# One attention, MoE and soft-MoE kernel: the decoding of w_out spread over two chunks, and a mask, a maximum and a scaling made one instruction

## The chip, the cores and the metric

The kernel runs on one core of one Trainium2 chip. TensorE (PE, with its weight loads shown apart as PEld), VectorE (DVE), ScalarE (ACT), GpSimd (POOL) and SyncE (SP, which here only issues DMAs) each work through their own list of instructions in order and meet at semaphores. The metric is the device time of one launch in microseconds, as the median of several runs.

## The reference, cut to what matters

Three stages follow each other, and the output of each is the input of the next:

```python
# 1. attention with a forget gate: B=4, H=8, S=576, D=64
scores = q @ k.T / sqrt(D)
cum = cumsum(log(clip(f, 1e-4, 1)))
scores = where(causal, -1e9, scores + cum[:, None] - cum[None, :])
attn = exp(scores - max(scores)); attn /= sum(attn) + 1e-9
x = attn @ v                           # as 2304 tokens x 512
# 2. MoE layer 1: w_in 512 x 2048, w_out 2048 x 512
h = x @ w_in
x = (h * sigmoid(1.702 * h)) @ w_out
# 3. soft MoE: phi 512 x 32; 8 experts of 4 slots, F = 1024
logits = x @ phi
d = softmax(logits, over tokens); slot_in = d.T @ x
slot_out = relu(slot_in @ w1[e]) @ w2[e]        # per expert
out = softmax(logits, over slots) @ slot_out
```

w_in and w_out arrive as 64-bit floats and are read as pairs of 32-bit words.

## The kernel before, in words

**Order.** The program is written with tiles from named pools; a tile that takes the place of an older one of the same tag waits until that one's last reader is done. A scheduler then sets the order of the instructions on each engine, from the program's order and its own model of durations, so that a change in pools or program order moves instructions on every engine.

**Attention** is cut into 20 rows: 4 batches by 5 blocks of queries, four of 128 queries and a last one of 64. Rows 0 to 4 (the first batch) find their maxima beforehand (`emit_max`, `emit_mrow`, whose transposed maxima go to the PSUM tile mT and by ACT L411 into the operand qa). Rows 5 to 19 are *late rows* (`emit_qk`): the block of scores `scs` in PSUM gets the causal mask by a DVE addition in place (L333), its maximum by a DVE reduction (L537), for the rows of 64 queries the larger of that and the diagonal block's maximum (L541), and the maximum is scaled, with its sign turned, by L542. ACT then takes the exponential `pf` (L545) and its f16 part (L554), DVE the remainder (L555). Both parts, `pn`, are turned by a DMA transpose into `ph`, and PE multiplies them with the values (pv, L594 to L596). There are 78 such units: 6, 12, 24 and 24 of the rows whose width is 1, 2, 3 and 4 blocks (a unit holds 4, 2, 1 and 1 heads), and 12 of the rows of 64 queries. DVE L608 scales to x, and x is turned to `xt` (L640 on ACT, L641 on DVE).

**Layer 1** goes over 9 chunks of 256 tokens, each of 8 *units* (`moe_steps`): 12 matmuls `hp` (L746 to L748), a tanh on ACT (L754), a DVE instruction (L755) to `g`. w_out is never multiplied with all tokens: it is folded with phi first (`fold_phi`: w_out's tile is transposed to woT, copied by ACT L234, multiplied with phi to wps by L237, copied by DVE L241 to wphi), and a `turn` makes logits from g: four transposes gT (L722), an ACT copy (L724), four matmuls p (L726). At the end of a chunk `slot_steps` gathers the slots (lg, d of L818, sp of L826).

**Decoding of a weight tile.** Raw words land in SBUF, POOL (L194) or ACT (L196) takes the high word, ACT (L197) the low one, and DVE joins them by L199 and L202. The 32 tiles (16 of w_in, 16 of w_out) are asked for by `more_w`, up to five tiles ahead in DMAs.

**After the attention** the expert weights (128 tiles of 256 KB) stream through a ring of SBUF slots.

Of the kernel before, what the change touches and what calls it, by code (L numbers as in the profile page):

```python
# [30 lines left out]
def attention_moe_softmoe(ctx, tc, q, k, v, f, w_in, w_out, phi, w1, w2, out):  # L31
# [192 lines left out]
    w_phi, wps = [], {}  # L224

    def fold_phi(ff):

# [7 lines left out]
        o = wps[0][:, ff % 4 * NS:(ff % 4 + 1) * NS]  # L235
        for kk in range(KD):
            nc.tensor.matmul(  # L237
                o, lhsT=wt_[:, kk * 128:(kk + 1) * 128], rhs=phi_sb[:, kk, :], start=(kk == 0), stop=(kk == KD - 1)
            )
        if ff % 4 == 3:  # L240
            nc.vector.tensor_copy(  # L241
                wphi[:, ff - 3:ff + 1, :], wps[0][:, 0:4 * NS].rearrange("p (f s) -> p f s", f=4)
            )
# [234 lines left out]
    def emit_diag(r):  # L478
# [21 lines left out]
        nc.vector.tensor_reduce(out=m2, in_=dg, axis=AX.X, op=ALU.max)  # L500
        DG[r] = dg, m2

    def emit_qk(r, u):
# [33 lines left out]
        nc.vector.tensor_reduce(  # L537
            out=mx, in_=sc[:, 0:hb * nb].rearrange("p (h n) -> p h n", h=hb), axis=AX.X, op=ALU.max
        )
# [618 lines left out]
```

## Time and profile before

| quantity | value |
|---|---|
| time, median of 3 runs | 623.53 us (618.25 to 632.64) |
| span of the profiled execution | 615.8 us; its own time is not printed |
| lowest and median time above that span | 2.45 and 7.73 us |
| PE busy | 533.6 us (87%) |
| DVE busy | 377.4 us (61%) |
| ACT busy | 308.6 us (50%) |
| POOL busy | 67.9 us (11%) |

The page's span is what the profiler saw of one execution from the first instruction to the last, and the time of a run holds some microseconds around it. The program falls into stages: up to 64 us the loads and the first attention rows; 64 to 160 the first chunk of layer 1 with the folding of w_out; 160 to 465 the late attention rows with chunks 1 to 6; 465 to 545 the end of layer 1; 545 to the end the experts. The engine's busy time is read by stage, since each stage has another limit.

### The profile page before, as it was taken

The numbers are of one execution on the slowest core, as the hardware profiler recorded it, in microseconds if no ns is written. First come the engines' busy times: TensorE is split into PE (matmuls) and PEld (weight loads), VectorE is DVE, ScalarE is ACT, GpSimd is POOL, SyncE is SP. The second block draws the span as 40 slices with busy tenths as digits, with TensorE's granted clock in tenths as the row PEclk, the third lists the DMA queues.
The fourth block names the chain that finished last, engine by engine and source line by source line (L and its number), as shares of the span: only waits on it lengthen the run. The fifth ranks groups of instructions, "written<-read, shape, count | busy, mean of one in ns | idle before, by whom it ended". The sixth has DMA issues, their size and how long they took to land.

```text
span 615.8 us, 13848 instructions
## 1 busy us (share of the span) xinstructions
PE 533.6 (87%) x5447; PEld 335.1 (54%) x5447; DVE 377.4 (61%) x971; ACT 308.6 (50%) x603; POOL 67.9 (11%) x120
## 2 busy tenths in 40 slices
PE   4477979899889899979999989988999999879971
PEld 3376667688545555655556565555664544323541
DVE  8989586649575767787586875777754352320131
ACT  5776384657654556656466564555652342211120
POOL 4756272120000000000000000000000000000000
PEclk9887998899989989989999998999998999869996
DMA  9966685439993536999744897955451399689999
GB/s 252 249 161 144 181 263 155 142 102 154 189 173 79 94 74 122 173 183 185 141 82 70 139 163 164 152 80 104 79 91 22 117 381 322 206 278 351 285 279 280
DMA packets 246497, 105.65 MB, mean 172 GB/s; under 512 B 202624, under 2 KB 234112, under 8 KB 246432
## 3 DMA queue, kind: packets, MB, share of 16 engines
q1 hardware_dynamic: 246432, 104.77, 73.6%
q8 instruction: 43, 0.70, 0.5%
q14 instruction: 22, 0.18, 0.1%
HBM read 64.63 MB, written 4.72 MB: 113 GB/s over the span
## 4 chain that ended last, share of the span: by engine, by line
PE 42%; DMA 8%; DVE 2%; ACT 1%; issue 1%; SPq 1%; DVEq 0%; ACTq 0%
PE hp L746 6%; PE hp L747 6%; PE hp L748 6%; PE gT L722 4%; DMA ph<-pn 4%; PE sp L826 3%; DMA we<-in_moe_w_dram 3%; PE l L1055 2%; PE p L726 2%; PE pv L594 2%; PE so L1077 1%; PE scs L516 1%; PE scs L517 1%; PE pv L595 1%; PE pv L596 1%; PE sw L857 1%
## 5 line engine op out<-in xcount | busy, mean ns | idle before, releaser
L746 PE MATMUL hp<-w,xt 128*128 128x512 f16 x288 | 111.3, 386 | 0.0
L747 PE MATMUL hp<-w,xt 128*128 128x512 f16 x288 | 110.6, 384 | 0.0
L748 PE MATMUL hp<-w,xt 128*128 128x512 f16 x288 | 109.9, 382 | 0.0
L754 ACT ACTIVATE g<-hp 128x512 f32<-128x512 f32 x72 | 42.7, 593 | 75.4 <-PE hp L748 75.3
L755 DVE SCALAR_TENSOR_TENSOR g<-g,hp 128x512 f32<-128x512 f32 x72 | 49.1, 682 | 46.5 <-ACT g L754 46.2
L545 ACT ACTIVATE pf<-scs,mx 128x512 f32<-128x512 f32 (+3 forms) x108 | 54.8, 544 | 37.2 <-DVE mx L542 32.2
L555 DVE TENSOR_TENSOR pn<-pf,pn 128x512 f16<-128x512 f32 (+2 forms) x78 | 51.0, 655 | 25.3 <-ACT pn L554 24.8
L594 PE MATMUL pv<-vv,ph 128*128 128x65 f16 (+2 forms) x360 | 48.2, 201 | 11.0 <-DMA ph<-pn 6.9
L554 ACT ACTIVATE pn<-pf 128x512 f16<-128x512 f32 (+2 forms) x78 | 47.3, 608 | 17.3 <-DMA ph<-pn 16.1
L537 DVE TENSOR_REDUCE mx<-scs 128x1 f32<-128x512 f32 (+3 forms) x78 | 49.9, 642 | 3.0 <-PE scs L533 2.3
L722 PE MATMUL gT<-ident,g 128*128 128x128 f32 x288 | 48.3, 287 | 1.1 <-DVE g L755 1.1
L746 PEld LDWEIGHTS <-xt 128*128 128x128 f16 x288 | 28.6, 99 | 35.8 <-issue 13.9
L595 PE MATMUL pv<-vv,ph 128*128 128x65 f16 (+2 forms) x360 | 47.3, 198 | 0.0
L594 PEld LDWEIGHTS <-ph 128*128 128x128 f16 (+2 forms) x360 | 35.0, 103 | 22.4 <-DMA ph<-pn 9.0
L596 PE MATMUL pv<-vv,ph 128*128 128x65 f16 (+2 forms) x360 | 46.9, 196 | 0.0
L748 PEld LDWEIGHTS <-xt 128*128 128x128 f16 x288 | 28.4, 99 | 33.6 <-issue 2.8
L724 ACT COPY gt<-gT 128x512 f32<-128x512 f32 x72 | 41.6, 582 | 7.5 <-PE gT L722 7.2
L516 PE MATMUL scs<-kab,qa 128*128 128x128 f16 x240 | 36.7, 225 | 6.2 <-ACT pf L545 5.6
L747 PEld LDWEIGHTS <-xt 128*128 128x128 f16 x288 | 28.6, 99 | 23.0 <-issue 2.1
L722 PEld LDWEIGHTS gT<-ident,g 128*128 128x128 f32 x288 | 34.0, 145 | 11.8 <-issue 4.2
L595 PEld LDWEIGHTS <-ph 128*128 128x128 f16 (+2 forms) x360 | 35.5, 104 | 3.3 <-issue 0.4
L517 PE MATMUL scs<-kab,qb 128*128 128x128 f16 x240 | 36.5, 226 | 0.0
(198 smaller groups left out, 1048.6 us busy)
## 6 DMA issues: line engine op xcount, KB each, us to landing
we<-in_moe_w_dram SPq DMA_DIRECT2D x128, 256.0 KB, 5.5
raw<-in_moe_w_in_dram SPq DMA_DIRECT2D x16, 512.0 KB, 6.4
raw<-in_moe_w_out_dram SPq DMA_DIRECT2D x16, 512.0 KB, 4.6
kf<-in_k_dram SPq DMA_DIRECT2D x16, 256.0 KB, 3.5
qf<-in_q_dram SPq DMA_DIRECT2D x16, 256.0 KB, 4.2
out_dram<-ob SPq DMA_DIRECT2D x16, 256.0 KB, 4.0
vf<-in_v_dram SPq DMA_DIRECT2D x12, 256.0 KB, 3.6
ph<-pn SPq DMA_TRANSPOSE x78, 3.3
```

The source lines that it names most:

```text
L537: nc.vector.tensor_reduce(out=mx, in_=sc[:, 0:hb * nb].rearrange("p (h n) -> p h n", h=hb), axis=AX.X, op=ALU.max)
L545: nc.scalar.activation(out=pf[:, hh * nb:(hh + 1) * nb], in_=sc[:, hh * nb:(hh + 1) * nb], func=AF.Exp, bias=mx[:, hh:hh + 1], scale=SC,)
L554: nc.scalar.activation(out=pn[:, 0, 0:w], in_=pf, func=AF.Copy)
L555: nc.vector.tensor_tensor(out=pn[:, 1, 0:w], in0=pf, in1=pn[:, 0, 0:w], op=ALU.subtract)
L594: nc.tensor.matmul(o, lhsT=ph[0:rr, 0, off:off + n], rhs=vh, start=(j == 0), stop=False)
L595: nc.tensor.matmul(o, lhsT=ph[0:rr, 0, off:off + n], rhs=vl, start=False, stop=False)
L596: nc.tensor.matmul(o, lhsT=ph[0:rr, 1, off:off + n], rhs=vh, start=False, stop=(j == i))
L722: nc.tensor.transpose(pt[:, a * 128:(a + 1) * 128], g[:, a * 128:(a + 1) * 128], ident)
L746: first = nc.tensor.matmul(hp, lhsT=xt[:, 0, kk, ts], rhs=win(0, fg, kk), start=(kk == 0), stop=False)
L747: nc.tensor.matmul(hp, lhsT=xt[:, 0, kk, ts], rhs=win(1, fg, kk), start=False, stop=False)
L748: nc.tensor.matmul(hp, lhsT=xt[:, 1, kk, ts], rhs=win(0, fg, kk), start=False, stop=(kk == KD - 1))
L755: nc.vector.scalar_tensor_tensor(out=g, in0=g, scalar=1.0, in1=hp, op0=ALU.add, op1=ALU.mult)
```

## The change

- *w_out.* Chunk 0 asks for four weight tiles per unit up to its fourth unit as before (16 tiles, all of w_in), and from there for two per unit: 18, 20, 22, 24. Units 0 to 3 of chunk 1 ask for the other eight, two each. Loads are issued up to 7 tiles ahead rather than 5.
- *Turns* may begin as soon as the four tiles of w_out that they need are folded (`folded`), rather than when all are.
- *Folding* gathers two tiles: wps lies in the three `mm` buffers of PSUM rather than in the single `mi` one, and 8 copies of 128x64 to wphi take the place of 4 of 128x128. mT moves to `mm` as well.
- *SBUF.* w_out's decoded tiles lie in eight pairs o0 to o7 (the same bytes as before). Some raw tiles of w_out land in pairs that are still empty (`RAW_AT`) rather than in the ring `g`; the first rows' k and q lie in o7 to o5; the low words have a ring of two of their own, `low`, where they shared `gt` of three.
- *Late rows.* One DVE instruction per head (`tensor_tensor_reduce`, L556 of the new kernel) adds the mask, scales by minus 1/8 and takes the minimum, writing the scaled scores back in place and the minimum to mx; for the rows of 64 queries it starts from the diagonal's maximum, which `emit_diag` has scaled. It replaces L333, L537, L541 and L542. The mask becomes a tile `zmq` of 128x640, zeros ahead of the causal part. The exponential is taken with scale -1, pn's f16 part with the factor 256 by ACT, and its remainder by a DVE scalar_tensor_tensor (L569) rather than a tensor_tensor.

The core of the diff:

```diff
-    W_AHEAD = 5
+    W_AHEAD = 7
+    N_LOW = 2
+    RAW_AT = (7, 6, 5, 4, 3, None, None, 7, 6, None, None, 7, None, None, None, None)
...
-            raw = w_raw[n] = mp.tile([128, c], src.dtype, tag="g", name="raw", bufs=N_G)
+            at = None if which == "in" else RAW_AT[a]
+            if at is None:
+                raw = w_raw[n] = mp.tile([128, c], src.dtype, tag="g", name="raw", bufs=N_G)
+            else:
+                raw = w_raw[n] = wp.tile([128, c], src.dtype, tag=f"o{at}", name="raw")
...
-        low = mp.tile([128, 512], U32, tag="gt", name="low", bufs=N_GT)
+        low = ap_.tile([128, 512], U32, tag="low", name="low", bufs=N_LOW)
...
-        if ff % 4 == 0:
-            wps[0] = ps_mi("wps")
...
+        wot.append(wt_)
+        if len(wot) < 2:
+            return
+        wps = ps_mm("wps")[:, 0:2 * NS].rearrange("p (f s) -> p f s", s=NS)
...
+        nc.vector.tensor_copy(wphi[:, ff + 1 - 2:ff + 1, :], wps)
+        wot.clear()
+        folded[0] = (ff + 1) // 4
...
-        pt = ps_mi("mT")
+        pt = ps_mm("mT")
...
-            if r >= 5:
-                mask_in(sc[:, 0:w].rearrange("p (h n) -> p h n", h=hb)[:, :, 128 * i:], mqk)
...
-        nc.vector.tensor_reduce(
-            out=mx, in_=sc[:, 0:hb * nb].rearrange("p (h n) -> p h n", h=hb), axis=AX.X, op=ALU.max
-        )
-        if n < 128:
-            nc.vector.tensor_tensor(out=mx, in0=mx, in1=DG[r][1][:, u], op=ALU.max)
-        nc.vector.tensor_scalar(out=mx, in0=mx, scalar1=-SC, scalar2=math.log(PB), op0=ALU.mult, op1=ALU.add)
+        mask = zmq[:, 640 - nb:640] if n == 128 else zmq[:, 0:nb]
...
+            nc.vector.tensor_tensor_reduce(
+                out=o, in0=o, in1=mask, scale=-SC, scalar=3.0e38 if n == 128 else DG[r][1][:, u],
+                op0=ALU.add, op1=ALU.min, accum_out=mx[:, hh:hh + 1],
+            )
...
-        nc.scalar.activation(out=pn[:, 0, 0:w], in_=pf, func=AF.Copy)
-        nc.vector.tensor_tensor(out=pn[:, 1, 0:w], in0=pf, in1=pn[:, 0, 0:w], op=ALU.subtract)
+        nc.scalar.activation(out=pn[:, 0, 0:w], in_=pf, func=AF.Copy, scale=PB)
+        nc.vector.scalar_tensor_tensor(
+            out=pn[:, 1, 0:w], in0=pf, scalar=PB, in1=pn[:, 0, 0:w], op0=ALU.mult, op1=ALU.subtract
+        )
...
-            if c == 0:
-                more_w(max(6, 4 * u + 4))
+            if c < 2:
+                more_w((max(6, 4 * u + 4) if u < 4 else 16 + 2 * (u - 3)) if c == 0 else 24 + 2 * u + 2)
...
-            if w_at[0] == NW:
-                for _ in range(min(3 if c < 2 else 2, len(turns) - 1)):
-                    turn(*turns.popleft())
+            for _ in range(min(3 if c < 2 else 2, len(turns) - 1)):
+                if turns[0][2] >= folded[0]:
+                    break
+                turn(*turns.popleft())
```

How the order of instructions moves is shown at three places. On DVE in the late rows, before, at two heads of width 4 (g is of layer 1):

```order
L755 SCALAR_TENSOR_TENSOR g<-g,hp 128x512
L333 TENSOR_TENSOR scs<-scs,mqk 128x128
L537 TENSOR_REDUCE mx<-scs 128x1
L542 TENSOR_SCALAR mx<-mx 128x1
L333 TENSOR_TENSOR scs<-scs,mqk 128x128
L537 TENSOR_REDUCE mx<-scs 128x1
L555 TENSOR_TENSOR pn<-pf,pn 128x512
L542 TENSOR_SCALAR mx<-mx 128x1
```

The same engine in the same rows now (the instruction is listed as ISA; a second one, which reads the accumulated minimum to mx, follows it):

```order
L771 SCALAR_TENSOR_TENSOR g<-g,hp 128x512
L556 ISA scs,mx<-scs,zmq 128x512
L556 ISA mx 128x1
L793 TENSOR_SCALAR l_2656<-p_2188 128x256
L619 TENSOR_SCALAR rd<-pv 128x4
L622 RECIPROCAL rd<-rd 128x4
L569 SCALAR_TENSOR_TENSOR pn<-pf,pn 128x512
L556 ISA scs,mx<-scs,zmq 128x512
L556 ISA mx 128x1
```

Three instructions of a unit have become two that always stand together; nothing stands between maximum and scaling any longer.

On PE in chunk 0, before, between attention and two of layer 1's units (woT and wps are w_out's folding):

```order
L589 MATMUL pv<-vv,pf 128x65 x16
L232 MATMUL woT<-ident,w_1183 128x128 x4
L232 MATMUL woT<-ident,w_1191 128x128 x4
L237 MATMUL wps<-phi_sb,woT 128x32 x8
L232 MATMUL woT<-ident,w_1211 128x128 x4
L746 LDWEIGHTS xt
...
L237 MATMUL wps<-phi_sb,woT 128x32 x4
L232 MATMUL woT<-ident,w_1230 128x128 x4
L232 MATMUL woT<-ident,w_1338 128x128 x4
L237 MATMUL wps<-phi_sb,woT 128x32 x8
L232 MATMUL woT<-ident,w_1358 128x128 x4
L232 MATMUL woT<-ident,w_1378 128x128 x4
L746 LDWEIGHTS xt
```

PE in chunk 0 now, at two places ahead of a unit (scs is attention of the first batch):

```order
L252 MATMUL wps<-phi_sb,woT 128x32 x4
L243 MATMUL woT<-ident,wo 128x128 x4
L762 LDWEIGHTS xt
L762 MATMUL hp<-w,xt 128x512
...
L449 LDWEIGHTS kab
L449 MATMUL scs<-qa,kab 128x64
L451 LDWEIGHTS kab
L451 MATMUL scs<-qb,kab 128x64
L252 MATMUL wps<-phi_sb,woT 128x32 x8
L243 MATMUL woT<-ident,wo 128x128 x4
L762 LDWEIGHTS xt
L762 MATMUL hp<-w,xt 128x512
```

By the end of chunk 0's last unit 60 of the 64 woT transposes stood in the list before; now 32 do, and the other 32 follow in units 0 to 4 of chunk 1. The number of matmuls is the same.

On SP, before, around the first raw tiles of w_out (kab, qa and qb are attention's transposes):

```order
L179 DMA raw<-in_moe_w_in_dram 128x1024 x4
L181 DMA raw<-in_moe_w_out_dram 128x1024 x3
L312 DMA_TRANSPOSE qa<-qan 128x8x64
L312 DMA_TRANSPOSE qb<-qbn 128x8x64
L181 DMA raw<-in_moe_w_out_dram 128x1024 x3
L274 DMA qf<-in_q_dram 128x8x64
L312 DMA_TRANSPOSE qa<-qan 128x8x128
L312 DMA_TRANSPOSE qb<-qbn 128x8x128
L181 DMA raw<-in_moe_w_out_dram 128x1024 x2
L274 DMA qf<-in_q_dram 128x8x64
L181 DMA raw<-in_moe_w_out_dram 128x1024 x8
```

SP now, from the load of phi on:

```order
L119 DMA phi_sb<-in_moe_phi_dram 128x4x32
L195 DMA raw<-in_moe_w_out_dram 128x1024 x4
L193 DMA raw<-in_moe_w_in_dram 128x1024 x5
L195 DMA raw<-in_moe_w_out_dram 128x1024
L290 DMA qf<-in_q_dram 64x8x64
L328 DMA_TRANSPOSE kab<-kbn 128x8x128
L328 DMA_TRANSPOSE kab<-kan 128x8x128
```

The first four raw tiles of w_out now stand ahead of five raw tiles of w_in and of the third row's transposes, where they stood behind them.

## Rows read from the trace of the kernel before

**Rows 1.** Windows by stage: length; busy of PE, PEld, DVE, ACT, POOL; clock, DMA, GB/s.

```profile
0.00:64.00 64.00, 38.31 (x361) 33.69 (x362) 57.08 (x105) 42.45 (x68) 38.17 (x56) 0.84 0.82 197
64.00:160.00 96.00, 87.17 (x828) 68.95 (x826) 62.83 (x122) 57.80 (x110) 25.27 (x33) 0.95 0.69 172
160.00:465.00 305.00, 284.73 (x3089) 173.90 (x3089) 216.45 (x599) 175.18 (x353) 3.94 (x30) 0.96 0.70 124
465.00:545.00 80.00, 72.89 (x537) 34.77 (x536) 29.07 (x116) 23.64 (x55) 0.53 (x1) 0.91 0.67 230
545.00:615.80 70.80, 50.45 (x636) 23.75 (x636) 12.02 (x30) 9.50 (x19) 0.00 (x0) 0.89 0.99 288
```

**Rows 2.** PE's waits, 64 to 160 us: us in total, times, longest.

```profile
PE scs L433 <- ACT qa L411: 2.2, 1, 2.2
PE wps L237 <- ACT woT L234: 1.7, 3, 1.2
...
PE wps L237 <- DVE wphi L241: 0.5, 1, 0.5
...
PE mT L409 <- DVE wphi L241: 0.4, 1, 0.4
```

**Rows 3.** PE's waits, 160 to 470 us.

```profile
PE pv L594 <- DMA ph<-pn: 6.9, 7, 1.7
PE scs L516 <- ACT pf L545: 5.6, 3, 2.6
PE d L818 <- ACT dT L810: 3.9, 3, 2.5
PE pv L594 <- DVE x L608: 2.8, 2, 1.4
```

**Rows 4.** Windows of 4 us behind two long waits of PE.

```profile
216.00:220.00 4.00, 3.81 (x27) 2.25 (x31) 3.09 (x16) 3.08 (x9) 0.00 (x0) 0.50 0.49 92
...
272.00:276.00 4.00, 2.66 (x23) 2.34 (x23) 3.94 (x19) 4.00 (x13) 0.00 (x0) 0.50 1.00 189
```

**Rows 5.** DVE's groups by form, whole span: busy us, mean ns, idle before.

```profile
L555 DVE TENSOR_TENSOR pn<-pf,pn 128x512 f16<-128x512 f32 x42 | 28.8, 686 | 13.5 <-ACT pn L554 13.3
...
L537 DVE TENSOR_REDUCE mx<-scs 128x1 f32<-128x512 f32 x36 | 24.6, 685 | 2.7 <-PE scs L533 2.3
L333 DVE TENSOR_TENSOR scs<-scs,mqk 128x128 f32<-128x128 f32 x48 | 13.8, 291 | 6.6 <-PE scs L517 6.4
...
L537 DVE TENSOR_REDUCE mx<-scs 128x1 f32<-128x384 f32 x24 | 13.1, 546 | 0.2
...
L542 DVE TENSOR_SCALAR mx<-mx 128x1 f32<-128x1 f32 x60 | 8.7, 147 | 0.7
...
L333 DVE TENSOR_TENSOR scs<-scs,mqk 128x256 f32<-128x256 f32 x12 | 5.1, 426 | 0.1
L333 DVE TENSOR_TENSOR scs<-scs,mqk 128x512 f32<-128x512 f32 x6 | 4.2, 692 | 0.4 <-PE scs L517 0.4
...
L142 DVE TENSOR_TENSOR_SCAN cum<-ones,fs 32x576 f32<-32x576 f32 x1 | 1.3, 1346 | 0.8 <-ACT fs L139 0.8
```

**Rows 6.** Line L319, 160 to 470 us: count, ns as min/median/max, first and last start.

```profile
L319 DVE SCALAR_TENSOR_TENSOR vv<-vf,vv x12: 673/688/697, 162.1 to 394.4; 128x512 f16<-128x512 f32 x9, 64x512 f16<-64x512 f32 x3
```

**Rows 7.** Timeline of DVE, then of ACT, 210 to 214.5 us: start, duration.

```profile
212.62 0.15 DVE L542 TENSOR_SCALAR mx<-mx 128x1 f32<-128x1 f32 x1
...
211.14 0.63 ACT L287 ACTIVATE qbn<-qf 128x512 f16<-128x512 f32 x1 [2.10 <-DMA qb<-qbn]
...
212.61 0.58 ACT L754 ACTIVATE g<-hp 128x512 f32<-128x512 f32 x1
213.27 0.69 ACT L545 ACTIVATE pf<-scs,mx 128x512 f32<-128x512 f32 x1
```

**Rows 8.** Folding on PE, groups by form, 64 to 160 us.

```profile
L237 PE MATMUL wps<-phi_sb,woT 128*128 128x32 f32 x128 | 16.9, 279 | 2.2 <-ACT woT L234 1.7 <-DVE wphi L241 0.5
```

**Rows 9.** SP's waits in its queue, 0 to 165 us.

```profile
SPq L181 <- ACT low L197: 32.8, 12, 6.7
```

More of the change, by code (lines that the diff above doesn't have):

```diff
@@ L76, in attention_moe_softmoe @@
     ident16 = const.tile([128, 128], F16, name="ident16")
-    mqk = ap_.tile([128, 128], BF16, name="mqk")
+    zmq = ap_.tile([128, 640], BF16, name="zmq")
+    mqk = zmq[:, 512:640]
     mkq = ap_.tile([128, 128], BF16, name="mkq")
@@ L98, in setup_consts @@
         nc.vector.tensor_copy(identb, ident)
-        nc.gpsimd.memset(mqk, 0.0)
+        nc.gpsimd.memset(zmq, 0.0)
         nc.gpsimd.affine_select(
@@ L161, in attention_moe_softmoe @@
     w_at, w_loaded = [0], [0]
-    W_AHEAD = 5
+    W_AHEAD = 7
+    N_LOW = 2
+    RAW_AT = (7, 6, 5, 4, 3, None, None, 7, 6, None, None, 7, None, None, None, None)
+    wo_pair = {}
     def w32_tile(n):
-        return wp.tile([128, 512], F32, tag=f"w{n + 1 if n < NI else n}", name="w32")
+        if n < NI:
+            return wp.tile([128, 512], F32, tag=f"w{n + 1}" if n < NI - 1 else "o0", name="w32")
+        ff = n - NI
+        if ff % 2 == 0:
+            wo_pair[ff // 2] = wp.tile([128, 2, 512], F32, tag=f"o{ff // 2}", name="wo")
+        return wo_pair[ff // 2][:, ff % 2]
     def w_load(n):
@@ L222, in more_w @@
             fold_phi(*w_phi.pop())
-    w_phi, wps = [], {}
+    w_phi, wot, folded = [], [], [0]
     def fold_phi(ff):
-        if ff % 4 == 0:
-            wps[0] = ps_mi("wps")
         pt = ps_mm("woT")
@@ L234, in fold_phi @@
         nc.scalar.copy(out=wt_, in_=pt)
[L235 to L238, printed above, removed]
-            )
[L240 to L243, printed above, removed]
+        wot.append(wt_)
+        if len(wot) < 2:
+            return
+        wps = ps_mm("wps")[:, 0:2 * NS].rearrange("p (f s) -> p f s", s=NS)
+        for n, wt_ in enumerate(wot):
+            for kk in range(KD):
+                nc.tensor.matmul(
+                    wps[:, n], lhsT=wt_[:, kk * 128:(kk + 1) * 128], rhs=phi_sb[:, kk, :], start=(kk == 0), stop=(kk == KD - 1)
+                )
+        nc.vector.tensor_copy(wphi[:, ff + 1 - 2:ff + 1, :], wps)
+        wot.clear()
+        folded[0] = (ff + 1) // 4
     def split_one(n):
@@ L255, in attention_moe_softmoe @@
     ROW = {r: j for j, r in enumerate(rows)}
-    nat = {}
+    nat, first_kq = {}, {}
     KA, KB, QA, QB, VV = {}, {}, {}, {}, {}
@@ L268, in load_row @@
             elif r < 3:
-                t = wp.tile([128, H, D], F32, tag=f"w{2 * KF - 1 - 2 * r - (nm == 'q')}", name=nm + "f")
+                if r not in first_kq:
+                    first_kq[r] = wp.tile([128, 2, 512], F32, tag=f"o{7 - r}", name="kqf")
+                t = first_kq[r][:, nm == "q"].rearrange("p (h d) -> p h d", h=H)
             else:
@@ L500, in emit_diag @@
         nc.vector.tensor_reduce(out=m2, in_=dg, axis=AX.X, op=ALU.max)
+        nc.vector.tensor_scalar(out=m2, in0=m2, scalar1=-SC, scalar2=None, op0=ALU.mult)
         DG[r] = dg, m2
@@ L536, in emit_qk @@
         mx = ap_.tile([128, 4], F32, tag="mx", name="mx", bufs=4)[:, 0:hb]
[L537 to L542 removed]
+        mask = zmq[:, 640 - nb:640] if n == 128 else zmq[:, 0:nb]
         pf = ap_.tile([128, w], F32, tag="pf", name="pf", bufs=2)
         for hh in range(hb):
+            o = sc[:, hh * nb:(hh + 1) * nb]
+            nc.vector.tensor_tensor_reduce(
+                out=o, in0=o, in1=mask, scale=-SC, scalar=3.0e38 if n == 128 else DG[r][1][:, u],
+                op0=ALU.add, op1=ALU.min, accum_out=mx[:, hh:hh + 1],
+            )
             nc.scalar.activation(
[L546 to L547 removed]
+                out=pf[:, hh * nb:(hh + 1) * nb], in_=o, func=AF.Exp, bias=mx[:, hh:hh + 1], scale=-1.0
             )
@@ L912, in ring_tile @@
         ring.append(slot)
-        if tag in ("xt", "g"):
+        if tag in ("xt", "g") or tag[0] == "o":
             if not pair:
@@ L1007, in attention_moe_softmoe @@
                     ring.extend([(mp, "g", N_G)] * (2 * (N_G - 2)))
-                    ring.extend([(wp, f"w{p}", 1) for p in range(NI, NW)])
+                    ring.extend([(wp, f"o{p // 2}", 1) for p in range(KF)])
                     load_e(4)
```

3 lines of the change are left out of this document (1 added, 2 removed).

## The prediction

> **What bounds the kernel now.** I read the stages first [rows 1]. PE is the busiest engine in each until 545 us; DVE reaches 62.83 of 96 us in the second stage and 216.45 of 305 us in the third, ACT less. So PE's list sets the time, and what can be won is PE's idle time and what its clock loses. Idle is 96 - 87.17 = 8.8 us in the second stage, 305 - 284.73 = 20.3 in the third. The last stage has a DMA share of 0.99: there the expert weights set the pace.
>
> Second, who ends PE's waits. In the second stage one wait stands out, 2.2 us for qa, and some 2.6 us belong to the folding: wps for ACT's copy 1.7, wps and mT for the single `mi` buffer until DVE has copied wphi 0.5 and 0.4 [rows 2]. In the third the waits are few and long: 6.9 us for transposed ph, 5.6 for pf (a score block not yet freed), 3.9 for dT, 2.8 for x [rows 3]. Third, the clock: in the 4 us that follow the waits at 212 and 270 us PE is granted 0.50 of full speed, its lower level of 1.2 GHz, with PE busy 3.81 and 2.66 of 4 us [rows 4]. The stages' clocks [rows 1] price that: 0.05 x 87.17 = 4.4 us in the second stage, 0.04 x 284.73 = 11.4 in the third.
>
> A profiled span of 615.8 us is the base. The fastest run is 2.45 us above it, the median 7.7. I make the sum on the span and add 7.7.
>
> **The change part by part.**
>
> *Up to 64 us: 0, ends -3 and +3.* w_in is still asked for four tiles per unit. Four raw tiles of w_out now go ahead of five of w_in and of row 3's transposes on SP, which may delay those; in return the loads no longer wait for the low words, for which SP's queue stood 32.8 us in 12 waits [rows 9]. POOL's mask tile is five times as wide, early and beside loads. I let these cancel. No row prices either; the nearest is qa's wait of 2.2 us [rows 2], so with a margin 3 us each way.
>
> *64 to 160 us: -3, ends -10 and +4.* The folding costs PE 16.9 us for 128 wps matmuls [rows 8], 1.1 us for each of 16 tiles, beside the tile's transposes. It is not removed: half of it moves to chunk 1 and so gives nothing by itself. What it can give is waits. The wait for qa is behind ACT's decoding instructions: in the changed order that ACT instruction follows the row's exponential instead of two decodes; I take 1.2 of its 2.2 us. The `mi` waits, 0.5 + 0.4, go, since wps and mT have three buffers; of the 4.4 us of clock I take 1. Sum 3.1. Against it, wps now takes turns with hp, woT and gT in `mm`: eight pairs waiting the 0.5 us that a copy cost before would lose 4, the upper end. The lower end is three quarters of the stage's idle and clock loss, 8.8 + 4.4. The decode work of DVE is no shorter, and in the new list all 32 joins still stand ahead of the eighth g. So "spread" is true of PE's folding only.
>
> *160 to 465 us: -4.5, ends -17 and +20.* Removed per unit are mask, maximum, scaling [rows 5]. The new instruction reads PSUM and a bf16 tile and writes PSUM, the same streams as the masking of 128x512 at 692 ns; so I price 512 columns at 0.692, 384 at 0.55 (maximum 0.546), 256 at 0.426, 128 at 0.291, and its accumulator read at 0.147 like the other 128x1 instructions. Per unit: width 1: 0.692 + 0.683 + 0.160 (wide maximum and four-column scaling, near the rows shown) = 1.535 becomes 4 x 0.438 = 1.752; width 2: 0.426 + 0.681 + 0.157 = 1.264 becomes 2 x 0.573 = 1.146; width 3: 0.291 + 0.546 + 0.147 = 0.984 becomes 0.697; width 4: 0.291 + 0.685 + 0.147 = 1.123 becomes 0.839; 64 queries: 0.685 + 2 x 0.15 = 0.985 becomes 0.839, and three small extra scalings cost 0.5. With 6, 12, 24, 24 and 12 units: +1.3 - 1.4 - 6.9 - 6.8 - 1.8 + 0.5 = -15.1 us of DVE.
>
> DVE is not the bound, so this counts only where a unit's chain ends late. The chain is 0.28 us shorter for widths 3 and 4. Seven waits for ph x 0.28 = 2.0; three for dT, whose DVE part queues behind late units, x 0.28 = 0.8; with the waits shorter, some 15% of the 11.4 us of clock, 1.7. Sum 4.5. Not the waits for pf: in the one at 213 us the scaling came at 212.62 behind row preparation, but ACT's own list (qbn at 211.14, pn, tanh at 212.61) reached the exponential only at 213.27 [rows 7]; that wait is ACT's and stays. Eight tiles' folding now lies in chunk 1, 8 x 1.1 us of wps moved: fill for waits, and no loss. The lower end takes two thirds of the four waits' 19.2 us and of the clock's 11.4 a third; the upper end is the second rival's, and without it 0.
>
> The remainder of pn becomes a scalar_tensor_tensor with an f32 and an f16 source in SBUF. Row preparation has that instruction with those kinds at 688 ns for 512 columns [rows 6], against 686 for the present tensor_tensor [rows 5]: 0. The Trainium skill speaks against this edit: "Vector Engine (DVE) Microarchitecture Reference", section 7, Points that are easy to get wrong, says that this form, with two SBUF sources that are not bf16, runs at half throughput. By that rule the sum would be the third rival's; the row contradicts it for these operands.
>
> *After 465 us: 0.* The last stage waits for DMA at 0.99 [rows 1]; the ring has as many slots. It moves rigidly with the end of attention, so what is won earlier is kept.
>
> Sum: -3 - 4.5 = -7.5, a span of 608.3, and with 7.7 above it **616 us**. The measurement can tell about 2% from no change, 12.5 us: faster is below 611, slower above 636.
>
> **The rivals.**
>
> *Waits and clock largely vanish* (598 to 611). A wait costs twice, in idle time and in the slow clock behind it [rows 4]. If the shorter chains keep PE from idling at all in a few of these places, half of the 29.1 us idle and half of the 15.8 us of clock go: -22.4, 601. For it: the waits are few, 15 us of DVE's work go, and PE has 9 us of movable fill. Against it: the waits shown are ended by DMA and ACT, which get no faster. Chance 0.30.
>
> *Slower: the new instruction runs at the rate of the scan* (636 to 645). It keeps a running minimum, as the scan L142 keeps a running sum: 1346 ns for 576 columns [rows 5]. The maxima of 512 and 384 columns, 685 and 546 ns, give 755 for that width: 1.78 times. Then 512 columns take 1.235, 384 0.985, 256 0.76, 128 0.52; the 15 us won become 28 lost, and each chain of width 3 and 4 is 0.26 us longer with DVE at 245 of 305 us. Were a quarter of a microsecond to show in each of 78 units, +20, 636 on the span and 643 in all. It decides from 1.0 us per 512 columns, where the chain becomes longer than now. For it: the trace shows no such instruction, and it does three operations in one pass. Against it: the maximum of 512 columns also keeps a running value, at 685 ns [rows 5]. Chance 0.12.
>
> *Slower: pn's remainder at half rate* (650 to 670). Were the 78 remainders of the new form to take twice as long, 512 columns 1.37 us instead of 0.686, DVE would have 78 x some 0.6 = 47 us more and every chain 0.6 us; with three quarters of it on the path, 623.5 + 35 = 659. It decides from about 1 us per 512 columns. This is what the Trainium skill's rule above would do. Against it stands the row of 688 ns [rows 6]. Chance 0.02.
>
> *It does not do what it says* (618 to 628). The joins still all stand before the eighth g, so w_out's decoding is not spread on DVE, and DVE is off the path: then nothing moves. Chance 0.07.
>
> **The numbers.** Forecast 0.49, the others 0.30, 0.12, 0.02, 0.07. The forecast's own range is 606 to 624. The range 598 to 630 holds it, the first rival and the last, and leaves out the two slower ones, 0.14, and a little of the far ends. Faster by over 2%: 0.30, the first rival. Slower: 0.14. Within: 0.49 + 0.07 = 0.56.
>
> **What would show it.** L556 at about 0.69 us for 512 columns with a 0.15 read behind it, L569 at 0.69, DVE some 15 us less busy; waits of wps and mT for wphi gone, qa's wait near 1 us, ph's waits at some 5 us; the second stage some 3 us shorter, attention ending some 7 us earlier, the last stage as long as before. It is wrong if L556 takes over 1 us, if L569 takes about twice 0.69, if a wait for an `mm` buffer appears before wps, hp or gT, if w_in or row 3's transposes land later behind w_out's raw tiles, or if the waits in the third stage stay while DVE is less busy.

## The result and the profile after

The changed kernel takes **602.46 us** (median, 601.70 to 603.99), where the kernel before takes 624.09 (618.25 to 632.64) beside it: a ratio of 0.968 (95% interval 0.963 to 0.974). It is faster by 21.6 us. The forecast of 616 had the sign and its range held the time, but it forecast a third of the gain; the time lies where the first rival, waits and clock largely vanish, had put it (598 to 611).

The profiled execution has a span of 601.2 us, against 615.8, so these two executions differ by 14.6 us only. The missing 7 us are in the base: where both are known, an execution's time is mostly 1.7 to 1.9 us above its own span (2.4 at most), and the profiled execution of before was one of its quickest. The comparisons leave out executions over 1.5% above the quickest of the same kernel beside them, and so rest on 25 of the 51 executions of before. These have spans from 611.7 us, at a mean granted clock of 0.939, to 629.7 at 0.907; a line through all falls by 5.0 us for each 0.01 of clock (correlation -0.91).

The page's first line of the changed kernel (busy us and share of the span by engine):

```profile
PE 524.9 (87%) x5447; PEld 331.0 (55%) x5447; DVE 356.6 (59%) x960; ACT 310.9 (52%) x603; POOL 69.7 (12%) x120
```

As many PE instructions are busy 8.7 us less, at a mean granted clock of 0.940 against 0.931, and PE is idle 5.9 us less (76.3 of the span against 82.2). DVE is busy 20.8 us less. The fused instruction and pn's remainder, groups by form:

```profile
L569 DVE SCALAR_TENSOR_TENSOR pn<-pf,pn 128x512 f16<-128x512 f32 x42 | 28.8, 688 | 16.1 <-ACT pn L568 15.7
L556 DVE CUSTOM_DVE_ANT_0 scs<-scs,zmq 128x512 f32<-128x512 f32 x24 | 16.7, 697 | 6.9 <-PE scs L534 6.9
...
L556 DVE DVE_READ_ACCUMULATOR2_ANT mx<- 128x1 f32 x108 | 15.0, 139 | 0.0
...
L556 DVE CUSTOM_DVE_ANT_0 scs<-scs,zmq 128x384 f32<-128x384 f32 x24 | 13.4, 562 | 0.6 <-PE scs L534 0.5
...
L556 DVE CUSTOM_DVE_ANT_0 scs<-scs,zmq 128x256 f32<-128x256 f32 x24 | 10.1, 431 | 1.1 <-PE scs L534 0.8
...
L556 DVE CUSTOM_DVE_ANT_0 scs<-scs,zmq,m 128x512 f32<-128x512 f32 x12 | 9.0, 752 | 3.9 <-PE scs L548 3.8
...
L556 DVE CUSTOM_DVE_ANT_0 scs<-scs,zmq 128x128 f32<-128x128 f32 x24 | 7.1, 294 | 2.9 <-ACT pf L560 1.7 <-PE scs L534 1.0
```

697, 562, 431 and 294 ns where 692, 550, 426 and 291 were taken, and 139 for the read instead of 147: together 71.3 us, in place of the 86.6 of mask, maxima and scaling. The scan's rate is refuted, and so is the half rate for pn's remainder: 688 ns against 686 [rows 5]. On this the trace contradicts the Trainium skill's sentence on that form ("Vector Engine (DVE) Microarchitecture Reference", Points that are easy to get wrong) for an f32 and an f16 source.

PE's waits, which answer to [rows 2] and [rows 3], from 64 to 160 us and then from 160 to 470 us:

```profile
PE woT L243 <- DVE g L771: 1.7, 1, 1.7
PE pv L605 <- ACT pf L471: 1.1, 2, 0.7
PE pv L605 <- DVE x L624: 0.9, 1, 0.9
PE scs L449 <- DVE mt L369: 0.7, 1, 0.7
PE wps L252 <- ACT woT L245: 0.6, 1, 0.6
...
PE pv L610 <- DMA ph<-pn: 4.6, 5, 1.4
PE scs L533 <- ACT pf L560: 3.3, 4, 1.2
PE d L835 <- ACT dT L827: 2.4, 3, 1.1
PE scs L534 <- DMA qb<-qbn: 1.9, 1, 1.9
```

In these stretches qa's wait and the waits for wphi are gone; the long waits of 2.5 and 2.6 us for dT and pf are now 1.1 and 1.2.

**Where the time went.** Windows at fixed times compare different work, because the folding has moved. So I cut at a milestone of attention: the start of DVE's part of xt (L641 before, L657 now) for the 4th, the 9th and the 18th block of 128 tokens. Before, then now (columns as in [rows 1]):

```profile
0.00:134.40 134.40, 101.09 (x935) 83.13 (x935) 100.54 (x182) 82.58 (x140) 62.67 (x79) 0.89 0.72 189
134.40:273.20 138.80, 126.22 (x1366) 81.60 (x1364) 98.18 (x263) 80.03 (x164) 2.23 (x24) 0.96 0.75 134
273.20:486.50 213.30, 203.01 (x2154) 122.30 (x2154) 145.67 (x416) 118.64 (x241) 2.48 (x16) 0.96 0.63 110
486.50:615.80 129.30, 103.23 (x998) 48.02 (x996) 33.05 (x116) 27.32 (x62) 0.53 (x1) 0.90 0.94 297
```

```profile
0.00:122.50 122.50, 88.31 (x882) 73.64 (x883) 98.50 (x184) 80.75 (x137) 64.84 (x79) 0.89 0.80 207
122.50:259.90 137.40, 130.99 (x1425) 87.29 (x1424) 89.33 (x268) 82.64 (x166) 2.27 (x24) 0.99 0.79 131
259.90:473.50 213.60, 202.04 (x2149) 120.84 (x2147) 135.50 (x396) 119.96 (x241) 2.10 (x16) 0.96 0.68 112
473.50:601.20 127.70, 103.52 (x998) 49.27 (x995) 33.32 (x116) 27.53 (x62) 0.53 (x1) 0.90 0.98 300
```

- First stretch: 11.9 us shorter, with 12.8 us less of PE work done in it. That is mostly postponed folding, not a gain.
- Second stretch: 1.4 us shorter, with woT and wps at 19.2 us of PE instead of 8.2. Eleven more microseconds of work fit in because PE's idle time falls from 12.6 to 6.4 us and its clock rises from 0.96 to 0.99. **Here the gain of this pair is made.**
- Third stretch, late rows throughout, with 10 us less of DVE: 213.3 and 213.6 us. No gain in this pair; e12 and e3 below differ here.
- Fourth: 1.6 us shorter.

To the ninth block the work of PE is all but the same (2301 and 2307 matmuls), in 273.2 us before and 259.9 now. Of these 13.3 us 8.0 are PE's busy time, so mostly clock, and 5.3 its idle time. The second stretch is where the folding, the first late rows and the ends of chunks 0 and 1 meet. The change also costs something early. PE's longest wait, DVE's instructions in it, and POOL's beside them:

```profile
63.58 0.27 PE L449 MATMUL scs<-qa,kab 128*128 128x128 f16 x1 [10.59 <-DVE mt L369]
```

```profile
58.34 1.64 DVE L213 SCALAR_TENSOR_TENSOR low<-w,low 128x512 uint32<-128x512 uint32 x1
60.02 2.63 DVE L216 SCALAR_TENSOR_TENSOR w<-w,low 128x512 uint32<-128x512 uint32 x1
...
62.85 0.67 DVE L369 TENSOR_REDUCE mt<-scm 128x1 f32<-128x512 f32 x1
...
59.40 1.59 POOL L307 TENSOR_TENSOR kbn<-kf,kbn 64x512 f16<-64x512 f32 x1
60.96 1.15 POOL L262 TENSOR_TENSOR w<-w,w 128x512 f16<-128x512 f32 x1
```

A maximum of row 3 stands in DVE's list behind five decodes, whose steps take up to 2.63 us beside POOL's work instead of 0.69. Before, PE waited once for these maxima, 1.8 us.

### The profile page after: what moved, and what is told of

It is laid out like the page before. It is cut to its first block, busy times and chain, and to the rows that moved or that the text cites. A ratio compares the mean times of both kernels' runs of the same rounds, so it can differ in the third digit from the quotient of the medians.

```text
span 601.2 us, 13796 instructions
## 1 busy us (share of the span) xinstructions
PE 524.9 (87%) x5447; PEld 331.0 (55%) x5447; DVE 356.6 (59%) x960; ACT 310.9 (52%) x603; POOL 69.7 (12%) x120
## 4 chain that ended last, share of the span: by engine, by line
PE 69%; DMA 11%; DVE 7%; ACT 5%; issue 3%; POOL 2%; SPq 2%; DVEq 0%; ACTq 0%; POOLq 0%
PE hp L762 9%; PE hp L763 9%; PE hp L764 9%; PE gT L738 6%; PE sp L843 4%; PE p L742 4%; DMA ph<-pn 3%; PE pv L605 3%; PE pv L610 3%; PE l L1072 3%; DMA we<-in_moe_w_dram 2%; PE wps L252 2%; PE scs L533 2%; PE scs L534 2%; PE pv L611 2%
## 5 line engine op out<-in xcount | busy, mean ns | idle before, releaser
L560 ACT ACTIVATE pf<-scs,mx 128x512 f32<-128x512 f32 (+3 forms) x108 | 58.1, 544 | 40.0 <-DVE mx L556 32.6
L569 DVE SCALAR_TENSOR_TENSOR pn<-pf,pn 128x512 f16<-128x512 f32 (+2 forms) x78 | 51.0, 657 | 28.3 <-ACT pn L568 27.5
L610 PE MATMUL pv<-vv,ph 128*128 128x65 f16 (+2 forms) x360 | 48.6, 201 | 6.4 <-DMA ph<-pn 4.6
L556 DVE CUSTOM_DVE_ANT_0 scs<-scs,zmq 128x256 f32<-128x256 f32 (+3 forms) x96 | 46.8, 496 | 11.4 <-PE scs L534 9.2
L611 PE MATMUL pv<-vv,ph 128*128 128x65 f16 (+2 forms) x360 | 48.4, 198 | 0.0
L612 PE MATMUL pv<-vv,ph 128*128 128x65 f16 (+2 forms) x360 | 48.1, 197 | 0.0
L610 PEld LDWEIGHTS <-ph 128*128 128x128 f16 (+2 forms) x360 | 35.6, 104 | 17.7 <-issue 7.9
L611 PEld LDWEIGHTS <-ph 128*128 128x128 f16 (+2 forms) x360 | 36.0, 105 | 3.4 <-issue 1.0
L612 PEld LDWEIGHTS <-ph 128*128 128x128 f16 (+2 forms) x360 | 36.1, 106 | 1.0 <-issue 0.4
L533 PE MATMUL scs<-kab,qa 128*128 128x128 f16 x240 | 33.5, 219 | 3.3 <-ACT pf L560 3.3
```

The costliest lines, as they stand in the source:

```text
L556: nc.vector.tensor_tensor_reduce(out=o, in0=o, in1=mask, scale=-SC, scalar=3.0e38 if n == 128 else DG[r][1][:, u], op0=ALU.add, op1=ALU.mi ...
L560: nc.scalar.activation(out=pf[:, hh * nb:(hh + 1) * nb], in_=o, func=AF.Exp, bias=mx[:, hh:hh + 1], scale=-1.0)
L569: nc.vector.scalar_tensor_tensor(out=pn[:, 1, 0:w], in0=pf, scalar=PB, in1=pn[:, 0, 0:w], op0=ALU.mult, op1=ALU.subtract)
L610: nc.tensor.matmul(o, lhsT=ph[0:rr, 0, off:off + n], rhs=vh, start=(j == 0), stop=False)
L611: nc.tensor.matmul(o, lhsT=ph[0:rr, 0, off:off + n], rhs=vl, start=False, stop=False)
L612: nc.tensor.matmul(o, lhsT=ph[0:rr, 1, off:off + n], rhs=vh, start=False, stop=(j == i))
```

## The experiments

Theory 1 at first: the fusion makes the gain, in the late rows. Theory 2: the spreading of w_out makes it. All ratios are to the kernel before, measured beside each kernel on the same chip: a median of 627.1 us beside e1 to e4, 624.2 beside e5 to e8, 624.1 beside e9 to e12 and 625.2 beside e13 to e16. "Medians" is the ratio of the medians of all executions; where it and the ratio differ, the difference is a measure of how far a ratio can be trusted. "Full" is the span times the granted clock, a rough estimate of the time that a full clock would leave (it treats waits as if they shrank with the clock too), and "lost" the rest of the span, as means over the executions compared; for before, 571 to 573 and 46 to 54 us.

| kernel | spread | fused | median us | ratio (interval) | medians | full | lost |
|---|---|---|---|---|---|---|---|
| the change | yes | yes | 602.46 | 0.968 (0.963 to 0.974) | 0.965 | 565 | 36 |
| e13 the change again | yes | yes | 599.80 | 0.964 (0.956 to 0.971) | 0.959 | 561 | 38 |
| e1 fusion alone | no | yes | 614.38 | 0.979 (0.973 to 0.985) | 0.980 | 570 | 42 |
| e2 change unfused | yes | no | 607.61 | 0.968 (0.961 to 0.974) | 0.969 | 566 | 40 |
| e3 change, four tiles a unit | no | yes | 611.15 | 0.972 (0.965 to 0.979) | 0.975 | 569 | 39 |
| e12 both undone | no | no | 615.91 | 0.991 (0.987 to 0.995) | 0.987 | 573 | 41 |
| e5 storage and loads alone | no | no | 623.92 | 0.997 (0.993 to 1.002) | 1.000 | 576 | 45 |
| e6 folding and turns alone | no | no | 632.40 | 1.010 (1.006 to 1.014) | 1.013 | 578 | 52 |
| e7 e6 and two tiles a unit | yes | no | 612.19 | 0.975 (0.968 to 0.982) | 0.981 | 572 | 38 |
| e4 change, lead 3100 | yes | yes | 609.22 | 0.973 (0.966 to 0.980) | 0.972 | 571 | 35 |
| e8 before, lead 3100 | no | no | 624.69 | 1.009 (1.002 to 1.016) | 1.001 | 577 | 46 |
| e9 loads five ahead | yes | yes | 610.35 | 0.980 (0.972 to 0.989) | 0.978 | 571 | 37 |
| e10 60 matmuls, first place | yes | yes | 606.07 | 0.975 (0.968 to 0.983) | 0.971 | 568 | 37 |
| e11 DVE load, ran early | yes | yes | 614.54 | 0.985 (0.975 to 0.996) | 0.985 | 568 | 44 |
| e14 DVE load in late rows | yes | yes | 608.58 | 0.978 (0.970 to 0.986) | 0.973 | 567 | 40 |
| e15 120 matmuls in the wait | yes | yes | 601.91 | 0.966 (0.959 to 0.974) | 0.963 | 568 | 32 |
| e16 w_in later | yes | yes | 613.04 | 0.986 (0.973 to 0.999) | 0.981 | 569 | 43 |

**e1, fusion alone.** The hunks of `emit_qk`, `emit_diag` and `zmq`, put into the kernel before:

```diff
...
-        nc.vector.tensor_reduce(
...
+            nc.vector.tensor_tensor_reduce(
...
```

> The kernel before with the late rows' fused instruction alone; w_out decoded, folded and stored as before. If the late rows' shorter DVE chain makes the gain (theory 1: fewer long waits of PE from 160 to 390 us, and with them fewer half-clock stretches there), this is 609 to 614 us. If the spreading of w_out makes it (theory 2), this stays at 619 to 625 with DVE 15 us less busy. By the forecast's own sum it would be 4.5 us faster than before.

614.38 us, 0.979. Theory 1 said 609 to 614 and theory 2 619 to 625: it lies near the first, so the fusion can give some 60% of the gain without any spreading.

**e2, the change unfused.**

```diff
...
+        nc.vector.tensor_reduce(
...
-            nc.vector.tensor_tensor_reduce(
...
```

> The changed kernel with mask, maximum and scaling as four instructions again: the spreading of w_out, its storage and its PSUM buffers alone. Theory 1 expects 617 to 621 us: at the same amount of PE work done the changed kernel was 4 us ahead when its late rows began. Theory 2 expects 602 to 608. If the two parts only work together, both this and the fused instruction alone stay within 6 us of before.

0.968: by the ratio the whole gain, without the fusion; by time 607.61 us against 602.46 and, on the same chip, 599.80 (e13). Each part alone gives more than half of the gain, and their gains, 2.1% and 3.2%, together exceed the change's 3.2 to 3.6%. So neither theory stands alone, and the parts overlap.

**e3, four tiles a unit again**, all else as changed:

```diff
-            if c < 2:
-                more_w((max(6, 4 * u + 4) if u < 4 else 16 + 2 * (u - 3)) if c == 0 else 24 + 2 * u + 2)
+            if c == 0:
+                more_w(max(6, 4 * u + 4))
```

> The changed kernel with all of w_out asked for in chunk 0 again, four tiles per unit; storage, PSUM buffers, loads seven ahead, early turns and the fused instruction stay. If it is the two tiles per unit that help in the first 160 us, this gives back some 4 us, 605 to 608; if storage and PSUM buffers do, it stays at 601 to 604; if the folding in chunk 1 matters as fill for the late rows, 608 to 614.

0.972. By the ratios 0.4 to 0.8% is given back, by the medians 0.9 to 1.5%, not clear of the intervals: how much the spreading is worth beside the fusion isn't shown.

**e4, another order of the same instructions.**

```diff
-    P_PV, P_XT, P_MG, P_W, P_MG2 = (1.2, 2.4, 3000, 5, 8000)
+    P_PV, P_XT, P_MG, P_W, P_MG2 = (1.2, 2.4, 3100, 5, 8000)
```

> The changed kernel with attention's lead over layer 1 set to 3100 instead of 3000 in the program's order: no instruction is added or removed, about a fifth of PE's list is in another order. If the gain comes from the parts of the change, this stays within 3 us of the changed kernel. If it comes from how the order happens to fall, it moves by 5 us or more, and differences of that size between the other kernels prove nothing.

0.973: the full-clock part is 6 to 10 us longer than the change's. How the order falls is worth 0.5 to 0.9%; a difference of that size between two kernels here need not come from what an edit was meant to do.

**e5, storage and loads alone; e6, folding by pairs and early turns alone; e7, e6 with two tiles a unit.** In short:

```diff
 e5, against before
-    W_AHEAD = 5
+    W_AHEAD = 7
...
+    RAW_AT = (7, 6, 5, 4, 3, None, None, 7, 6, None, None, 7, None, None, None, None)
...
 e6, against before
...
-            wps[0] = ps_mi("wps")
...
+        wps = ps_mm("wps")[:, 0:2 * NS].rearrange("p (f s) -> p f s", s=NS)
...
+                if turns[0][2] >= folded[0]:
 e7, against e6
-                more_w(max(6, 4 * u + 4))
+                more_w((max(6, 4 * u + 4) if u < 4 else 16 + 2 * (u - 3)) if c == 0 else 24 + 2 * u + 2)
```

> The kernel before with the change's storage and loads alone: raw tiles of w_out partly in empty pairs, low words in their own ring, loads seven ahead. Folding into the one mi buffer by four tiles, turns after the last tile, and the late rows stay as before. If the loads of w_in and w_out that no longer wait for the low words (32.8 us of SP's waits before) make the spreading's gain of 3%, this is at 0.970 to 0.978 of before. If the folding and the early turns do, it is at 0.99 to 1.00.

> The kernel before with the folding by pairs into mm, mT in mm and the early turns alone; storage, loads, four tiles per unit and the late rows as before. If folding and turns make the spreading's gain: 0.970 to 0.978 of before. If the storage and loads do: 0.99 to 1.00.

> As the last, and two tiles per unit into chunk 1 as in the change: the whole change without its storage, loads and fused instruction. The g ring then holds raw tiles longer beside layer 1's g, so by the storage theory this is at or above the time of folding and turns alone, 0.99 to 1.01 of before; by the theory that any spreading of PE's folding gives fill it is at 0.968 to 0.975.

0.997, 1.010 and 0.975. Storage and loads alone give nothing, though the 32.8 us for which SP's loads waited [rows 9] are 8.7 us there: taking that waiting away gains nothing. Folding with early turns alone loses 1%. Two tiles a unit turn that into a gain: 632.40 to 612.19 us, the largest effect of one edit, and without the change's storage. But only 4.3 of the 20.7 us between the two profiled executions are idle time of PE (88.9 and 84.6 us). The other 16.4 are busy time of the same number of matmuls, and 9.8 of these lie behind the ninth block, where no folding is left (e6, then e7):

```profile
285.10:502.60 217.50, 205.48 (x2154) 124.59 (x2154) 146.16 (x417) 119.22 (x241) 2.10 (x16) 0.95 0.64 108
```

```profile
276.00:482.50 206.50, 195.71 (x2146) 119.43 (x2147) 143.69 (x415) 116.24 (x239) 2.10 (x16) 0.99 0.62 112
```

So most of this gain is clock (0.95 and 0.99 here), and why the clock is higher so far from the folding no run shows.

**e8, the kernel before in another order**, the edit of e4 in the kernel before.

> The kernel before with attention's lead over layer 1 set to 3100 instead of 3000: no instruction more or less, another order of PE's list. If the kernel before owes its low granted clock to how its order happens to fall, this is 1% or more away from it in either direction; if the gain belongs to the parts of the change, it is within 0.5%. Said before: the same edit of the changed kernel stood at 0.973 of before, against 0.968 for the changed kernel.

1.009 (1.002 to 1.016), and 1.001 by the medians: this other order doesn't make the kernel before quicker, and what its order is worth lies between nothing and 0.9%.

**e12, both undone**: e2 with the edit of e3.

> The changed kernel with four tiles per unit in chunk 0 and with mask, maximum and scaling apart: storage, loads, folding by pairs and early turns alone. Storage alone stood at 0.997 and folding with turns alone at 1.010 of before. If two tiles per unit are what made 0.9675 without the fusion, this is at 0.985 to 1.00; if storage and folding together make it, 0.968 to 0.975.

0.991. This closes the square. Without the fusion the spreading takes 0.991 to 0.968, with it 0.972 to 0.968 or 0.964; the fusion takes 0.991 to 0.972 without the spreading, 0.968 to 0.968 or 0.964 with it. So by the ratios the second part adds little to the first. By the medians it adds nearly what it gives alone: the spreading 1.8% without the fusion and 0.9 to 1.5 with it, the fusion 1.2% without the spreading and 0.4 to 1.0 with it. With intervals of 0.4 to 0.8% either way, how far the parts overlap stays open. The second stretch (block 4 to block 9) and the third, of e12, of e3 and of e2:

```profile
121.50:269.80 148.30, 132.29 (x1394) 86.31 (x1394) 95.67 (x259) 78.24 (x161) 2.15 (x24) 0.95 0.72 125
269.80:485.00 215.20, 202.27 (x2154) 122.20 (x2154) 146.79 (x415) 118.70 (x241) 2.10 (x16) 0.97 0.64 109
```

```profile
122.80:265.00 142.20, 131.30 (x1403) 86.64 (x1402) 87.42 (x263) 79.02 (x161) 2.15 (x24) 0.98 0.73 127
265.00:472.90 207.90, 196.97 (x2149) 119.40 (x2147) 135.68 (x395) 119.57 (x241) 2.10 (x16) 0.98 0.70 115
```

```profile
120.60:263.10 142.50, 131.98 (x1424) 88.69 (x1423) 98.03 (x264) 82.58 (x169) 2.26 (x24) 0.97 0.76 132
263.10:474.60 211.50, 200.66 (x2146) 120.67 (x2147) 146.51 (x414) 118.51 (x239) 2.10 (x16) 0.97 0.65 109
```

PE's idle time in the second stretch is 16.0 us with neither part (12.6 in the kernel before), 10.9 with the fusion, 10.5 with the spreading, 6.4 with both; the clock is 0.95, 0.98, 0.97 and 0.99. These savings of idle time nearly add: 5.1 and 5.5 apart, 9.6 together. In the third stretch e3 is 7.3 us shorter than e12, but the change (213.6 us, and 211.6 in e13) isn't shorter than e2 (211.5), so what the fusion gives there is not settled. What PE waits for in the second stretch, in e12 and then in the changed kernel:

```profile
PE d L834 <- ACT dT L826: 6.8, 2, 4.6
PE lg L798 <- DVE l L792: 1.9, 1, 1.9
PE p L741 <- ACT gt L739: 1.8, 1, 1.8
```

```profile
PE pv L610 <- DMA ph<-pn: 2.3, 3, 0.9
PE woT L243 <- DVE g L771: 1.7, 1, 1.7
PE pv L610 <- DVE x L624: 0.8, 1, 0.8
```

In e12 the last decoding step starts at 120.2 us and the last folding matmul at 143.6 us. Behind them, at 157 to 213 us, PE comes to the ends of chunks 0 and 1 (lg, d, p) with nothing else to do while DVE and ACT are at the late rows and their preparation. The waits of d for dT, 6.8 us, are gone in e3 and in e2 alike, so here both parts take away the same wait. That the fusion does it by a shorter DVE list and the spreading by folding to do in the meantime (in e2 the last transposes for it start at 164 us) is read from the traces and was not tested apart.

**e9, loads five ahead.**

```diff
-    W_AHEAD = 7
+    W_AHEAD = 5
```

> The changed kernel with loads five tiles ahead instead of seven. In its trace PE stands idle for 10.6 us at 53 us, behind a maximum that waits in DVE's list behind five decodes; in the order of this kernel three decodes stand there. If that wait is on the path, 4 to 6 us less than the changed kernel: 0.959 to 0.962 of before. If what comes later hides it, 0.966 to 0.970.

0.980 (0.972 to 0.989), no better. The wait that it aimed at is 9.0 us long with three decodes ahead, where the changed kernel has 10.6 and in a second execution (e13) 8.9 with five; the count of decodes ahead does not set it. Behind the three decodes a copy of 64x24 (L305) took 3.60 us.

**e10 and e15, is it idle time that lowers the clock?** e10 put 60 matmuls behind row 0's maxima, ahead of the wait meant; e15 put 120 right in front of row 1's mT:

```diff
...
+                if fn == emit_mrow and args == (1,):
+                    warm(120)
```

> The changed kernel with 60 matmuls that nobody reads, put behind row 0's maxima, where PE waits 7 us for DVE (from 23.5 us): PE's other work, its order and its waits stay. If the half-clock stretch that follows (27 to 37 us in the changed kernel) comes from PE having been idle, it goes or shrinks, the matmuls at 31 to 37 us take 0.22 instead of 0.31 us, and the time falls by 1 to 3 us; if the clock falls for another reason, the stretch stays and the time is the same or up to 3 us longer.

> The changed kernel with 120 matmuls that nobody reads in front of row 1's mT, where PE stands idle for 7 us from 23.5 us (the earlier kernel of this kind had them at another place). They last some 6.6 us at full clock. If idle time of PE lowers the granted clock, the half-clock stretch from 27 us goes or starts later, and the matmuls behind mT (0.31 us each in the changed kernel) take 0.22. If not, they keep 0.31. The time itself may stay, since DVE ends the next long wait at 63 us: 0 to 3 us less.

e10 tells nothing on the wait meant: its matmuls ran from 14 to 19 us, ahead of the wait. e15 hits the wait, from 23 to 29 us. Windows of the changed kernel (e13, measured beside it), then of e15:

```profile
23.50:31.00 7.50, 0.83 (x7) 0.43 (x4) 7.50 (x12) 4.12 (x8) 7.22 (x6) 0.63 1.21 207
31.00:37.00 6.00, 6.00 (x53) 6.00 (x54) 4.24 (x10) 4.05 (x7) 2.10 (x3) 0.61 1.00 394
37.00:45.00 8.00, 5.13 (x53) 4.61 (x50) 6.27 (x10) 4.27 (x7) 7.19 (x6) 0.84 1.00 352
```

```profile
23.50:31.00 7.50, 6.73 (x119) 6.55 (x117) 7.50 (x12) 3.56 (x6) 7.21 (x6) 1.00 1.10 252
31.00:37.00 6.00, 2.73 (x38) 2.65 (x36) 4.15 (x6) 3.75 (x6) 3.21 (x3) 0.85 1.02 371
37.00:45.00 8.00, 6.99 (x51) 6.66 (x49) 4.53 (x11) 4.67 (x9) 6.94 (x5) 0.50 1.16 316
```

With PE busy through the wait it keeps the full 2.4 GHz there and mostly behind it (0.85 against 0.61); the half clock comes after the next pause instead, 3.3 us idle of the 6. So at this place idle time is what costs clock, shown by an edit. It is not the whole rule: behind a shorter pause at 16 to 18.2 us the clock of the next 5.3 us was 0.68 in e13 and 1.00 in the change's other execution. The time stays (601.91 against 599.80 us): at this place DVE ends the next long wait.

**e11 and e14, DVE's load given back, beside the chain.**

```diff
 e11
+        nc.vector.tensor_tensor(out=junk, in0=ident, in1=ident, op=ALU.add)
 e14
+        nc.vector.tensor_tensor(out=junk, in0=pf[:, 0:128], in1=ident, op=ALU.add)
```

> The changed kernel with one addition of 128x128 per late unit on DVE, about 0.19 us x 78 = 15 us, whose result nobody reads: DVE is as busy as with mask, maximum and scaling apart, but the chain from scores to exponential stays as short. If the fusion works through DVE's load, the time rises by 3 to 6 us; if it works through the chain or not at all beside the spreading, it stays within 2 us of the changed kernel.

> The changed kernel with an addition of 128x128 on DVE behind each late unit's remainder, reading its pf, 78 in all, about 15 us: the load that the fusion took from DVE, put back where it was taken, beside the chain. (The earlier kernel of this kind ran its additions in the first 75 us, where they cost 10 us.) If the fusion works through DVE's load: 3 to 8 us slower than the changed kernel. If DVE's load in the late rows is covered: within 2 us.

e11's additions depend on nothing and ran from 5 to 91 us. They took 434 ns each, 33.9 us in all, and by the fourth block the kernel is 10.9 us behind the change (133.4 against 122.5 us). PE's longest wait grew from 10.6 to 15.1 us:

```profile
PE scs L449 <- DVE mt L369: 15.8, 2, 15.1
```

It says that DVE has no room at the start, and nothing on the late rows. e14 has DVE busy for 15.6 us more than e13 (372.6 against 357.0) and costs 8.8 us: "within 2 us" is refuted. The unfused e2 carries about as much DVE load (377.2 us) in the chain itself, and on the same chip it took 607.61 us, 7.8 more than e13; by the ratios it is only 0.4% behind e13, and e14 is 1.4%. That speaks for DVE's load, but the additions also moved about a fifth of PE's list, and e4 shows that another order alone can do 3 to 6 us, so how much of the 8.8 is load and how much is order stays open.

**e13, the change again.**

> The changed kernel once more, so that the next ones are compared with it on the same chip. 0.966 to 0.972 of before. Span times granted clock, the time that a full clock would leave, stood at 565 us for it and at 572 for before; the rest at 36 and 46 to 54. By the theory that most of the gain is clock, both differences come back, the second the larger.

0.964. Spans of 598.6 us on average at a clock of 0.937, against 621.5 at 0.918: full 561 and 571, lost 38 and 51. By this estimate 13 of the 23 us between them are clock, and 10 would be there at full clock too.

**e16, w_in later.**

```diff
-                more_w((max(6, 4 * u + 4) if u < 4 else 16 + 2 * (u - 3)) if c == 0 else 24 + 2 * u + 2)
+                more_w((6, 6, 8, 12, 14, 16, 18, 20, 24, 28, 30, 32)[min(11, 8 * c + u)])
```

> The changed kernel with w_in asked for later in chunk 0 (6, 6, 8, 12, 14, 16, 18, 20 tiles after units 0 to 7, then 24, 28, 30, 32 rather than 26 to 32): row 3's maxima on DVE then have five decodes ahead of them, as before, but none between them. If PE's waits for these maxima (13 us in the changed kernel) shrink by that, 2 to 5 us less than the changed kernel; if the decodes that move into chunk 1 collide with the late rows instead, 2 to 6 us more.

0.986: the waits for row 3's maxima did not shrink (12.1 against 10.8 us in e13), and the clock fell. The attempts at taking the early wait away (e9, e16) failed; no kernel here beats the change.

## Why the prediction was wrong

- **The step that failed: the clock.** "Of the 4.4 us of clock I take 1" and "some 15% of the 11.4 us of clock, 1.7" make 2.7 us. In the profiled pair the same number of matmuls is busy 8.7 us less, and by e13's estimate the clock is 13 us of the usual gain. It was mis-sized twice. The profiled execution, at 0.931, showed less loss than the usual one (0.921 in the middle of the 25). And the waits and the clock were priced as separate terms, though idle time can bring the clock down (e15): with half of the idle time of the second stretch went most of its clock loss.
- **The base.** "I make the sum on the span and add 7.7" took the distance from the span to the median for a constant. It is 1.7 us around the span, and 6 that go with a lower clock in the usual execution of before. The change's median is 1.3 us above its profiled span.
- **Waits: about the size.** 4.8 us were forecast; PE's idle time fell by 5.9 us in the profiled pair, and by at most the 10 us of e13's estimate. "Eight tiles' folding now lies in chunk 1 ...: fill for waits, and no loss" named a mechanism and gave it no price: where the fusion is missing, e6 to e7 shows 20 us for two tiles a unit and e12 to e2 11 to 14, of which e7's are for the most part clock.
- **Up to 64 us, "0, ends -3 and +3".** Wrong inside: PE's waits for row maxima (L369) grew from 1.8 to 13.0 us, and xt of the second block began at 66.1 instead of 62.8 us, 3.3 us later, just beyond the end given.
- **The late rows, -4.5.** The DVE sum was right (15.1 forecast, 86.6 - 71.3 - 0.5 = 14.8 measured), ph's waits fell to 4.6 (some 5 forecast), dT's to 2.4. But in the profiled pair the units after the ninth block gave no time (213.3 and 213.6 us), where e12 to e3 shows 7.3 us; whether the term holds is open. Of pf's waits, "That wait is ACT's and stays" does not hold for the change, where they fall from 5.6 to 3.3 us; with the fusion alone (e1) PE still waits 5.3 us for pf in its second stretch, so it was not the fusion that took them.
- **After 465 us: 0.** Right within 1.6 us.
- **The rivals.** The first one's price gave 601, near the time, but in part by luck: it took 14.5 us of idle time and 7.9 of clock off the profiled span, where 5.9 and 8.7 came, and the 7.7 us put on top, where 1.3 were due, made up for it. Its counter-argument, that the waits are ended by DMA and ACT, which get no faster, was the misreading: a wait also ends by PE having other work in front of it. The scan's rate and the half rate are refuted by prices (and the scan's 0.26 us for a chain of width 3 should read 0.985 + 0.147 - 0.984 = 0.15). "Does not do what it says" named the right fact, that DVE's joins are not spread: their last one starts at 124.4 us, before at 145.7, while the last transposes for the folding move from 147 to 165 us. Its conclusion was wrong: it is PE's folding that is spread.

Open: why the order alone can move the time by up to 0.9% (e4, e8), how far the two parts overlap and with it the share of each, why the clock rises where no folding is left (e7), and e14's 8.8 us.

## What to carry to other kernels

Two edits that shorten or fill the same waits need not add: before summing their gains, ask which wait each of them touches, try each alone, and compare by more than one measure before reading a difference of a percent. A wait of PE can be paid twice, as idle time and as slower clock behind it, so movable PE work that needs nothing just then is worth more in the gaps between stages than done early. And compare a profile's span with the granted clock of many executions before using its distance to the median as a constant.
